# Turning q and k of four head pairs with 32x32 VectorE transposes instead of TensorE, in a retimed order of steps

## The chip, the cores and the metric

The kernel runs on one core of one Trainium2 chip. The metric is the device time of one execution in microseconds (us); lower is better. The inputs lie in device memory when the clock starts, and the output is written back there.

## What is computed

Attention with a sliding window and a few sink keys, followed by a two-layer MLP. Shapes: q, k and v are 4 batches x 8 heads x 768 positions x 64 in 32-bit floats; the weights are 512 x 2048 and 2048 x 512 in 64-bit floats; the output is 3072 x 512.

```python
scores = scale * np.matmul(q, k.transpose(0, 1, 3, 2))      # scale = 1/8
keep = is_sink | in_window                                  # 4 sinks, window of 128
scores = np.where(keep, scores, -1000000000.0)
a = np.exp(scores - max); a = a / (sum + 1e-09)
x = np.matmul(a, v)                                         # heads side by side: 3072 x 512
h = x @ w_in
out = (h * sigmoid(h)) @ w_out
```

## The kernel before, in words

**Chunks and pairs.** The 3072 rows are cut into 8 chunks of 384 rows (half a batch, three blocks of 128). Attention for a chunk runs in four *pairs* of heads; pair `p` belongs to chunk `p // 4`, so pairs 0 to 3 make chunk 0's input to the MLP and pairs 4 to 7 make chunk 1's. The first two chunks are both first halves of a batch, and they (`FP=8`, so pairs 0 to 7) go through a path of its own in 32-bit floats; the functions of that path begin with `f_`. All later pairs use hi/lo splits in the fp32r type, in `q_prep`, `k_prep`, `scores` and so on; those functions are not touched.

**The float32 path of a pair**, with head `j` = 0 or 1:

- `f_load` (line 629): four DMAs on SyncE's queue bring q and k in as 128 positions by 64 columns, in runs of 256 bytes.
- `f_prep` (line 667): TensorE turns q and k with 128x128 transposes into the PSUM tiles `qt` and `kt` (L673, six per pair). ScalarE copies them into SBUF: `kT` (L684) and two halves of `qT` (L687). `qT` is one of two long-lived tiles, `qlf` for even pairs and `qdf` for odd ones, in which head j's 64 partitions hold q and the others zeros. VectorE copies eight sink columns into `kT` (L688). For pairs 4 to 7 `qt` and `kt` take two of the three PSUM banks with the tag `at`.
- `f_scores(p, j)`: three matmuls per head (L720, "s" below), each followed by a masked maximum on VectorE (L727) that writes the tile `pm`.
- `f_softmax(p, j)`: three exponentials on ScalarE (L742), a sum's reciprocal on VectorE (L746, L747), three scalings (L753, on ScalarE for all but the first pair).
- `f_ptrans(p, j)`: six TensorE transposes of the probabilities (L765 to L770, tiles `pa` and `pb`), copied out into `pTz` by ScalarE (L771, L776) and VectorE (L772, L774).
- `f_av(p, j)`: three matmuls with v (L788, tile `o`); behind the second head ScalarE and VectorE split the result into `xh` and `xl` (L795, L796), which is what the MLP reads.

**The MLP of a chunk** goes over 16 slices of 128 hidden columns. Slice `fc` has twelve matmuls (L852, tile `h`, two PSUM buffers), then `act` (ScalarE makes `gh` at L863 and `sg` at L864, VectorE `gl` at L866), then nine matmuls into three output banks (L878 to L880, tiles `out`). L863 needs another ScalarE table than L742, so going from the one to the other costs an ACT_TABLE_LOAD.

**Weights.** They come in as 64-bit words, in 32 tiles of 512 KB: four groups of eight (four of w_in, four of w_out), group g serving the hidden slices 4g to 4g+3 of every chunk. Each tile is turned into a 32-bit float by three VectorE passes (L41, L42, L43, tile `wcv`), rounded into the hi part by ScalarE (L826) and the lo part taken by VectorE (L828; the first few on GpSimd). The raw tiles share two buffers, and `wcv` shares its buffers with `gh` and `gl`. All of this lies in the first 140 us, over the attention of pairs 0 to 7 and chunk 0's MLP.

**What sets the order.** Each step is put into a list with a time from the table `OPT`, and the steps are recorded in the order of these times. One unit is one hidden slice of the MLP. `S` is the start of the MLP, `F1` the delay of pairs 4 to 7 behind it, `s1` their spacing, `f_p` the lead of `f_prep`, `f_pt` that of `f_ptrans`, `w[g]` the start of weight group g, `m0` chunk 0's offset of `act`, and `a` the offsets of the later pairs. A list scheduler then fixes each engine's queue; every engine works its own queue strictly in order, as does SyncE with its DMAs, which wait there for their buffers.

Of the kernel before, what the change touches and what calls it, by code (L numbers as in the profile page):

```python
# [8 lines left out]
F32 = mybir.dt.float32  # L9
# [11 lines left out]
NS = 8  # L21
SEG = 128 + NS
# [2 lines left out]


OPT = dict(
    S=7.901, s0=0.903, f_l=2.468, f_p=-1.643, f_v=3.079, f_sm=0.693, f_pt=0.795, f_av=0.251,
    tk=15.973, s1=1.65, F1=1.024, D0=2.076, w=[0.458, 8.623, 11.237, 18.573], wd=[0.85, 0.58,
    1.293, 0.67], wc=19.252, wcd=2.681, warm=7, wg=4, ord=1, edge=8, dua=15, adp=0, glp=0,  # L30
    ptv=7, fill=[0, 4, 0, 0, 1, 0, 0, 2], na=[2, 16], lod=[6, 32], nv=[0, 0], hid=[0, 0],
    ktd=[0, 0], a=dict(load=-3.44, q=0.257, k=-0.012, v=1.813, s=1.461, sd=0.613, sm=1.795,
    smd=0.605, pt0=2.725, st=3.866, pt1=3.355, av0=4.289, av1=4.669), m0=dict(act=0.108,
    m2=1.206), m=dict(act=1.068, m2=1.546), fin=0.927, FP=8,
)


# [132 lines left out]
def attn_moe_kernel(  # L170
# [11 lines left out]
    nc = tc.nc  # L182
    B, H, S, D = q.shape
# [5 lines left out]
    P = 128  # L189
    HP = H // 2  # L190
    CT = 384
    NTB = CT // P
# [37 lines left out]
    with ExitStack() as fast:  # L230
# [59 lines left out]
        zero = {}  # L290
# [341 lines left out]
        def f_load(p):  # L632
            c, b, half, hp = geo(p)
            s = st[p]
            for x in ("qn", "kn"):
                if p < HP and p % 2:
                    s[x] = p2.tile([P, NTB, 2, D], F32, tag="sg", name=f"{x}{p}")
                else:
                    s[x] = p1.tile([P, NTB + (x == "kn"), 2, D], F32, tag=x, name=f"{x}{p}")
            for x, src in (("qn", q), ("kn", k)):  # L640
                for j in range(2):
                    nc.sync.dma_start(
                        s[x][:, :NTB, j, :],
                        src[b, 2 * hp + j, 0:CT].rearrange("(t p) d -> p t d", p=P),
                    )

        def f_load_v(p):
            c, b, half, hp = geo(p)
# [10 lines left out]
        def bank(p, early, name):  # L659

            if p < HP:
                pool, tag = (ps_h, "h") if early == "h" else (ps_o, early)
            else:
                pool, tag = ps_a, "at"
            return pool.tile([P, 512], F32, tag=tag, name=f"{name}{p}")

        def f_prep(p):
            s = st[p]
            qt = bank(p, "o0", "qt")
            kt = bank(p, "o1", "kt")  # L670
            for src, dst in ((s["qn"], qt), (s["kn"], kt)):
# [311 lines left out]
        D0 = O["D0"]  # L983
# [51 lines left out]
```

## Time and profile before

| | |
|---|---|
| median of 2 runs | 723.79 us (722.8 to 724.79) |
| the profiled execution | 723.66 us, of which the span from first to last instruction is 721.8 us |
| TensorE (PE) busy | 705.0 us of the span, 98% |
| ScalarE (ACT) busy | 489.4 us, 68% |
| VectorE (DVE) busy | 481.3 us, 67% |
| GpSimd (POOL) busy | 281.5 us, 39% |
| granted TensorE clock | 0.998 of full speed |

A busy share is a mean over stages with different limits. For this change the stage from 40 to 150 us counts, in which pairs 4 to 7, chunk 0's MLP and the weight conversion run side by side. A matmul's shown duration holds its pipeline's depth too; what it costs TensorE in a row of others is the step from one start to the next.

### The profile page before, as it was taken

To read this page: it belongs to the slowest core of one execution; us is meant where nothing else is said; L and a number is where in the kernel's file an instruction comes from. 1 tells how busy PE (TensorE), PEld (TensorE's weight loads), DVE (VectorE), ACT (ScalarE), POOL (GpSimd) and SP (SyncE) were. 2 spreads that over 40 slices of the span, in tenths; PEclk is the share of its full clock that TensorE was granted. 3 is DMA by queue.
4 is the path that set the end of the run, shared out by engine and by line. 5 is a ranking of instruction groups with operands and counts; after the bars stand their busy time and mean duration, and the time that the engine had idled before them with its cause. 6 is when DMAs were issued, how large, how long until landed. Compare 5 with 4: busy or idle time off the path is not lost.

```text
span 721.8 us, 12275 instructions
## 1 busy us (share of the span) xinstructions
PE 705.0 (98%) x3842; PEld 624.1 (86%) x3842; DVE 481.3 (67%) x1323; ACT 489.4 (68%) x1165; POOL 281.5 (39%) x667
## 2 busy tenths in 40 slices
PE   6998999999999999999999999999999999999997
PEld 4676778798999999999999999999999999998986
DVE  5899767976776687667866777767866776731111
ACT  4889788786776777777666777777667876732112
POOL 3310000055655666444555455544554554430000
PEclk9999999999999999999999999999999999999999
DMA  7556546434522262114521353114412321001001
GB/s 180 176 154 186 148 112 173 151 84 107 147 43 40 70 187 63 22 39 138 138 41 27 84 166 66 35 34 120 136 27 41 106 58 35 1 1 45 0 1 46
DMA packets 141334, 61.86 MB, mean 86 GB/s; under 512 B 130001, under 2 KB 130001, under 8 KB 141265
## 3 DMA queue, kind: packets, MB, share of 16 engines
q1 hardware_dynamic: 140976, 61.04, 32.9%
q8 instruction: 31, 0.51, 0.3%
q14 instruction: 39, 0.31, 0.1%
q10 hardware_dynamic: 288, 0.00, 0.0%
HBM read 54.72 MB, written 6.29 MB: 85 GB/s over the span
## 4 chain that ended last, share of the span: by engine, by line
PE 81%; DMA 5%; DVE 5%; ACT 3%; POOL 2%; issue 2%; SPq 1%; DVEq 0%; POOLq 0%; ACTq 0%
PE h L852 32%; PE out L880 11%; PE out L879 11%; PE out L878 11%; PE o L575 4%; DMA wraw<-in_moe_w_in_dram 3%; PE o L788 2%; PE s L468 2%; PE s L464 2%; PE pt L520 2%; DMA wraw<-in_moe_w_out_dram 2%; PE o L591 1%; DVE wcv L43 1%; DVE wcv L42 1%; PE o L584 1%
## 5 line engine op out<-in xcount | busy, mean ns | idle before, releaser
L852 PE MATMUL h<-xh,winh 128*128 128x384 f32 x512 | 177.2, 346 | 0.0
L852 PE MATMUL h<-xh,winl 128*128 128x384 f32 x512 | 173.9, 340 | 0.0
L852 PE MATMUL h<-xl,winh 128*128 128x384 f32 x512 | 172.7, 337 | 0.0
L878 PE MATMUL out<-wouth,gh 128*128 128x512 f32 x384 | 153.2, 401 | 1.7 <-ACT gh L863 1.6
L879 PE MATMUL out<-woutl,gh 128*128 128x512 f32 x384 | 151.8, 396 | 0.5 <-DVE woutl L828 0.3
L880 PE MATMUL out<-wouth,gl 128*128 128x512 f32 x384 | 150.2, 396 | 0.0
L863 ACT ACTIVATE gh<-h 128x384 fp32r<-128x384 f32 x128 | 62.9, 492 | 104.4 <-PE h L852 100.7
L866 DVE TENSOR_TENSOR gl<-sg,gh 128x384 fp32r<-128x384 f32 x128 | 75.4, 589 | 87.2 <-ACT sg L864 84.9
L852 PEld LDWEIGHTS h<-xh,winh 128*128 128x128 f32 x512 | 96.3, 188 | 3.0 <-issue 0.9
L852 PEld LDWEIGHTS h<-xl,winh 128*128 128x128 f32 x512 | 96.5, 189 | 2.1
L852 PEld LDWEIGHTS h<-xh,winl 128*128 128x128 f32 x512 | 96.2, 188 | 0.5 <-issue 0.3
L880 PEld LDWEIGHTS out<-wouth,gl 128*128 128x128 f32 x384 | 71.8, 188 | 17.2 <-DVE gl L866 0.6
L878 PEld LDWEIGHTS out<-wouth,gh 128*128 128x128 f32 x384 | 72.2, 188 | 14.4 <-ACT gh L863 2.4
L879 PEld LDWEIGHTS out<-woutl,gh 128*128 128x128 f32 x384 | 72.1, 188 | 13.2 <-DVE woutl L828 1.3
L505 POOL TENSOR_SCALAR pm<-pm,r 128x128 f32<-128x128 f32 x144 | 61.5, 442 | 42.5 <-DVE r L490 39.2
L485 ACT ACTIVATE pm<-pm,mx 128x264 f32<-128x264 f32 (+1 forms) x144 | 70.6, 492 | 1.3 <-DVE mx L472 0.3
L440 POOL TENSOR_TENSOR vs<-vn,vs 128x256 fp32r<-128x256 f32 (+1 forms) x48 | 33.3, 695 | 91.4 <-ACT vs L438 78.2
L864 ACT ACTIVATE sg<-h 128x384 f32<-128x384 f32 x128 | 62.5, 488 | 0.5
L472 DVE CUSTOM_DVE_ANT_0 pm<-s,m 128x264 f32<-128x264 f32 (+1 forms) x144 | 52.9, 411 | 11.9 <-PE s L468 11.6
L600 DVE TENSOR_TENSOR x<-o,x 64x512 f32<-64x512 f32 x48 | 32.8, 683 | 35.5 <-ACT x L599 34.4
L419 POOL CAST ks<-ksA 128x24 fp32r<-128x24 f32 (+1 forms) x24 | 4.8, 201 | 131.7 <-PE s L468 73.0
L438 ACT CAST vs<-vn 128x256 fp32r<-128x256 f32 (+1 forms) x48 | 18.6, 388 | 50.1 <-PE o L584 49.6
(162 smaller groups left out, 1337.7 us busy)
## 6 DMA issues: line engine op xcount, KB each, us to landing
wraw<-in_moe_w_in_dram SPq DMA_DIRECT2D x16, 512.0 KB
wraw<-in_moe_w_out_dram SPq DMA_DIRECT2D x16, 512.0 KB
wchk<-in_moe_w_in_dram SPq DMA_DIRECT2D x16, 512.0 KB
wchk<-in_moe_w_out_dram SPq DMA_DIRECT2D x16, 512.0 KB
qn<-in_q_dram SPq DMA_DIRECT2D x96, 48.0 KB
kn<-in_k_dram SPq DMA_DIRECT2D x64, 64.0 KB
vn<-in_v_dram SPq DMA_DIRECT2D x32, 128.0 KB
out_dram<-ost SPq DMA_DIRECT2D x7, 512.0 KB
```

The source lines that it names most:

```text
L440: nc.gpsimd.tensor_tensor(vs[:, j0:, j, 1, :], vn[:, j0:, j, :], vs[:, j0:, j, 0, :], ALU.subtract)
L472: nc.vector.tensor_tensor_reduce(out=pm[:, t, off:], in0=sp[:, :w], in1=(m0, m1, m2)[min(blk, 2)], scale=-0.125, scalar=3.0e38, op0=ALU.ad ...
L485: nc.scalar.activation(x, x, AF.Exp, bias=mx[:, p, j * NTB + t : j * NTB + t + 1], scale=-1.0, accum_out=r[:, t : t + 1],)
L505: nc.gpsimd.tensor_scalar(x, x, r[:, t : t + 1], 1.0, ALU.mult, ALU.mult)
L600: nc.vector.tensor_tensor(x32[:, :n], o[0:64, :n], x32[:, :n], ALU.add)
L852: nc.tensor.matmul(hps[:, :CT], w[g][:, cc, fs], s[x], start=n == 0, stop=n == 3 * NCC - 1)
L863: nc.scalar.activation(gh, hps[:, :CT], AF.Silu)
L864: nc.scalar.activation(sg, hps[:, :CT], AF.Silu)
L866: eng.tensor_tensor(gl, sg, gh, ALU.subtract)
L878: nc.tensor.matmul(o, gh[:, ts_], wout_h[g][:, f], start=fc == 0, stop=False)
L879: nc.tensor.matmul(o, gh[:, ts_], wout_l[g][:, f], start=False, stop=False)
L880: nc.tensor.matmul(o, gl[:, ts_], wout_h[g][:, f], start=False, stop=fc == NFC - 1)
```

## The change

Pairs 4 to 7 (`ft=[4, 8]`) load q and k with eight DMAs instead of four, each of 32 partitions, so that a 32x32 block of q lies on 32 partitions; the runs are 128 bytes instead of 256. VectorE's transpose, which turns each 32x32 block by itself, then writes `kT` and the two halves of `qT` directly. The TensorE transposes, the PSUM tiles `qt` and `kt` and the three ScalarE copies of these pairs are gone, and the copy of the eight sink columns goes from VectorE to GpSimd. Pairs 0 to 3 keep the old preparation. The table of times has new numbers: among others `S` 7.901 to 8.269, `F1` 1.024 to 2.394, `f_p` -1.643 to -1.822, `f_pt` 0.795 to 0.73, `w[1]` 8.623 to 9.414, `m0`'s `act` 0.108 to 0.421.

```diff
 OPT = dict(
-    S=7.901, s0=0.903, f_l=2.468, f_p=-1.643, f_v=3.079, f_sm=0.693, f_pt=0.795, f_av=0.251,
-    tk=15.973, s1=1.65, F1=1.024, D0=2.076, w=[0.458, 8.623, 11.237, 18.573], wd=[0.85, 0.58,
+    S=8.269, s0=0.903, f_l=2.468, f_p=-1.822, f_v=3.079, f_sm=0.693, f_pt=0.73, f_av=0.251,
+    tk=15.766, s1=1.65, F1=2.394, D0=2.076, w=[0.458, 9.414, 11.237, 18.573], wd=[0.85, 0.58,
...
             for x, src in (("qn", q), ("kn", k)):
                 for j in range(2):
-                    nc.sync.dma_start(
-                        s[x][:, :NTB, j, :],
-                        src[b, 2 * hp + j, 0:CT].rearrange("(t p) d -> p t d", p=P),
-                    )
+                    if not OPT["ft"][0] <= p < OPT["ft"][1]:
+                        nc.sync.dma_start(
+                            s[x][:, :NTB, j, :],
+                            src[b, 2 * hp + j, 0:CT].rearrange("(t p) d -> p t d", p=P),
+                        )
+                        continue
+
+                    s[x, "b"] = s[x].rearrange("p t h d -> p (t h d)")[:, :CT]
+                    for e in range(2):
+                        to = slice(64 * j + 32 * e, 64 * j + 32 * e + 32)
+                        nc.sync.dma_start(
+                            s[x, "b"][to].rearrange("p (i d) -> p i d", d=32),
+                            src[b, 2 * hp + j, 0:CT, 32 * e : 32 * e + 32].rearrange(
+                                "(i t) d -> t i d", t=32
+                            ),
+                        )
...
         def f_prep(p):
             s = st[p]
+            if OPT["ft"][0] <= p < OPT["ft"][1]:
+                qT = zero["qd" if p % 2 else "ql"]
+                kT = p1.tile([P, NTB, SEG], F32, tag="x32" if p % 2 else "ks", name=f"kT{p}")
+                s["qT"], s["kT"] = qT, kT
+                nc.vector.transpose(
+                    kT[:, :, :P], s["kn", "b"].rearrange("p (t c) -> p t c", c=P)
+                )
+                for j in range(2):
+                    rows = slice(64 * j, 64 * j + 64)
+                    nc.vector.transpose(qT[rows, j], s["qn", "b"][rows])
+                nc.gpsimd.tensor_copy(kT[:, 1, P:], kT[:, 0, :NS])
+                return
```

The table changes each engine's queue at many places in the first 150 us. Three of them follow, as the built programs have them; the number behind a tile's name tells buffers apart, and in `s_1_0` or `pa_4` the digits are pair or head and part.

TensorE, around the first output slice of chunk 0, before (the row with `out_0` is the first matmul that waits for `gh` of slice 0):

```order
L720 MATMUL s_1_2_716<-kT_600,qlf 128x264
L765 MATMUL pa_4_793<-ident,pm_0_637 128x128
L766 MATMUL pa_4_793<-ident,pm_0_637 128x128
L768 MATMUL pb_0_794<-ident,pm_0_637 128x128
L767 MATMUL pa_4_793<-ident,pm_0_637 8x128
L769 MATMUL pb_0_794<-ident,pm_0_637 128x128
L770 MATMUL pb_0_794<-ident,pm_0_637 128x128
L720 MATMUL s_0_0_841<-kT_662,qdf 128x128
L720 MATMUL s_0_0_841<-kT_662,qdf 128x256
L878 MATMUL out_0_750<-wouth_133,gh_0_698 128x512
```

The same place after the change, where `o_915` is pair 4's first product with v and `pa_4_951`, `pb_1_952` are the probabilities of its second head:

```order
L744 MATMUL s_0_2_890<-kT_681,qdf 128x264
L812 MATMUL o_915<-pTz_151,vn_616 64x384
L812 MATMUL o_915<-pTz_151,vn_616 64x256
L812 MATMUL o_915<-pTz_151,vn_616 64x128
L789 MATMUL pa_4_951<-ident,pm_1_753 128x128
L790 MATMUL pa_4_951<-ident,pm_1_753 128x128
L791 MATMUL pa_4_951<-ident,pm_1_753 8x128
L792 MATMUL pb_1_952<-ident,pm_1_753 128x128
L793 MATMUL pb_1_952<-ident,pm_1_753 128x128
L794 MATMUL pb_1_952<-ident,pm_1_753 128x128
L902 MATMUL out_0_715<-wouth_133,gh_0_676 128x512
```

More of pair 4's attention now stands ahead of the first output slice.

VectorE, around pair 4's first maxima, before (`wcv` is a weight tile, `s_0_0_638` pair 4's first scores):

```order
L688 COPY kT_600<-kt_593 128x8
L43 SCALAR_TENSOR_TENSOR wcv_0_631<-wraw_0_629,wcv_0_631 128x512
L828 TENSOR_TENSOR woutl_134<-wcv_7_607,wouth_133 128x512
L796 TENSOR_TENSOR xl_617<-o_577,xh_616 128x384
L828 TENSOR_TENSOR winl_136<-wcv_0_631,winh_135 128x512
L727 ISA pm_0_637,mx<-s_0_0_638,m_94 128x128
```

After the change, where the transposes of pair 5 (`qdf`) already stand between pair 4's steps:

```order
L852 TENSOR_TENSOR woutl_134<-wcv_7_588,wouth_133 128x512
L690 STREAM_TRANSPOSE qdf<-qn_627 64x384
L820 TENSOR_TENSOR xl_598<-o_571,xh_597 128x384
L751 ISA pm_0_666,mx<-s_0_0_667,m_94 128x128
L751 ISA mx 128x1
L41 TENSOR_SCALAR wcv_0_621<-wraw_0_619 128x512
L751 ISA pm_0_666,mx<-s_0_0_667,mf 128x256
```

The first tile of weight group 1 (`wcv_0`) went from ahead of pair 4's maxima to between them.

SyncE's queue, from the load of pair 4's v on, before:

```order
L654 DMA vn_620<-in_v_dram 128x3x64 x2
L802 DMA wraw_0_629<-in_moe_w_in_dram 128x1024
L802 DMA wraw_1_646<-in_moe_w_in_dram 128x1024
L642 DMA qn_623<-in_q_dram 128x3x64 x2
L642 DMA kn_624<-in_k_dram 128x3x64 x2
L802 DMA wraw_2_667<-in_moe_w_in_dram 128x1024
```

And after:

```order
L666 DMA vn_616<-in_v_dram 128x3x64 x2
L652 DMA qn_627<-in_q_dram 32x12x32 x2
L826 DMA wraw_0_619<-in_moe_w_in_dram 128x1024
L652 DMA qn_627<-in_q_dram 32x12x32
L652 DMA kn_628<-in_k_dram 32x12x32 x4
L826 DMA wraw_1_637<-in_moe_w_in_dram 128x1024
L826 DMA wraw_2_658<-in_moe_w_in_dram 128x1024
```

Pair 5's loads are twice as many, in smaller blocks, and stand partly ahead of the weight tiles that they followed.

More of the change, by code (lines that the diff above doesn't have):

```diff
@@ L27 @@
 OPT = dict(
-    S=7.901, s0=0.903, f_l=2.468, f_p=-1.643, f_v=3.079, f_sm=0.693, f_pt=0.795, f_av=0.251,
-    tk=15.973, s1=1.65, F1=1.024, D0=2.076, w=[0.458, 8.623, 11.237, 18.573], wd=[0.85, 0.58,
+    S=8.269, s0=0.903, f_l=2.468, f_p=-1.822, f_v=3.079, f_sm=0.693, f_pt=0.73, f_av=0.251,
+    tk=15.766, s1=1.65, F1=2.394, D0=2.076, w=[0.458, 9.414, 11.237, 18.573], wd=[0.85, 0.58,
     1.293, 0.67], wc=19.252, wcd=2.681, warm=7, wg=4, ord=1, edge=8, dua=15, adp=0, glp=0,
     ptv=7, fill=[0, 4, 0, 0, 1, 0, 0, 2], na=[2, 16], lod=[6, 32], nv=[0, 0], hid=[0, 0],
-    ktd=[0, 0], a=dict(load=-3.44, q=0.257, k=-0.012, v=1.813, s=1.461, sd=0.613, sm=1.795,
-    smd=0.605, pt0=2.725, st=3.866, pt1=3.355, av0=4.289, av1=4.669), m0=dict(act=0.108,
-    m2=1.206), m=dict(act=1.068, m2=1.546), fin=0.927, FP=8,
+    ktd=[0, 0], a=dict(load=-3.44, q=0.257, k=-0.36, v=1.782, s=1.198, sd=0.6, sm=1.795,
+    smd=0.605, pt0=2.69, st=3.866, pt1=3.355, av0=4.346, av1=5.057), m0=dict(act=0.421,
+    m2=1.206), m=dict(act=1.068, m2=1.546), fin=0.93, FP=8, ft=[4, 8],
 )
```

## The prediction

> **What bounds the kernel now.** I read the page first, then the span cut into stages, then who waits for whom where TensorE has gaps, and last the order in time there.
>
> ```profile
> PE   6998999999999999999999999999999999999997
> DVE  5899767976776687667866777767866776731111
> ACT  4889788786776777777666777777667876732112
> ```
>
> TensorE is busy nearly throughout, so the end moves by TensorE's work and by its gaps, and the gaps lie in the first fifth. There VectorE and ScalarE come nearest to full. The windows (busy us of each engine, count in brackets, granted clock, DMA share, GB/s) show it by stage:
>
> ```profile
> core 0: us, PE busy (x) PEld busy (x) DVE busy (x) ACT busy (x) POOL busy (x), PEclk, DMA share, GB/s
> 0.00:42.30 42.30, 34.75 (x172) 24.45 (x172) 32.00 (x123) 28.87 (x86) 15.69 (x27) 0.96 0.61 165
> 42.30:64.40 22.10, 19.80 (x108) 15.09 (x106) 19.84 (x57) 19.37 (x46) 0.00 (x0) 1.00 0.71 192
> 64.40:152.30 87.90, 86.73 (x443) 70.04 (x444) 69.11 (x173) 73.15 (x165) 4.78 (x11) 1.00 0.51 142
> 152.30:650.00 497.70, 497.03 (x2794) 455.19 (x2793) 349.86 (x954) 352.57 (x836) 261.07 (x629) 1.00 0.30 73
> ```
>
> Stage A is 42.3 to 64.4 us, from the first MLP matmul to the output matmuls of hidden slice 1. Stage B goes on to those of slice 15, at 152.3. In A three engines are each busy for 19.4 to 19.8 of 22.1 us: a chain through all three, with ScalarE what TensorE waits for:
>
> ```profile
> PE out L878 <- ACT gh L863: 1.6, 2, 1.1
> PE pa L765 <- ACT pm L753: 0.6, 1, 0.6
> ```
>
> From 152.3 on TensorE is busy for 497.03 of 497.70 us. The order of its rows there is the same in both programs but for one exchanged pair, so I add nothing behind B. Ahead of A TensorE's order differs only in pairs 2 and 3, whose transposes stand three matmuls earlier.
>
> **The change part by part.** First the prices on TensorE, from starts in the timeline:
>
> ```profile
> 31.31 1.27 PE L720 MATMUL s<-kT,qlf 128*128 128x128 f32 x6
> 32.64 1.51 PE L788 MATMUL o<-pTz,vn 128*64 128x384 f32 x6
> 34.08 0.33 PE L765 MATMUL pa<-ident,pm 128*128 128x128 f32 x1
> 52.91 0.49 PE L673 MATMUL qt<-ident,qn 128*128 128x128 f32 x3
> 53.24 0.49 PE L673 MATMUL kt<-ident,kn 128*128 128x128 f32 x3
> 53.57 0.60 PE L720 MATMUL s<-kT,qlf 128*128 128x128 f32 x3
> 60.58 0.34 PE L852 MATMUL h<-xh,winh 128*128 128x384 f32 x1
> 60.76 0.34 PE L852 MATMUL h<-xl,winh 128*128 128x384 f32 x1
> 70.94 0.40 PE L878 MATMUL out<-wouth,gh 128*128 128x512 f32 x1
> 71.18 0.39 PE L879 MATMUL out<-woutl,gh 128*128 128x512 f32 x1
> ```
>
> Three transposes step by 0.33, so 0.11 each; a hidden matmul 0.175, an output one 0.235, the scores of a head 1.2 (1.33 shown to the next start, of which I give some 0.1 to the change to another kind of matmul), a product with v 1.44, a group of six probability transposes 0.65.
>
> *Removed from TensorE:* 24 transposes x 0.11 = 2.6 us, half of them in A and half in B, where TensorE itself sets the pace.
>
> *Removed from ScalarE, added to VectorE:*
>
> ```profile
> L684 ACT COPY kT<-kt 128x384 f32<-128x384 f32 x4 | 1.9, 476 | 0.0
> L687 ACT COPY qdf<-qt 64x384 f32<-64x384 f32 x4 | 1.9, 474 | 0.0
> L687 ACT COPY qlf<-qt 64x384 f32<-64x384 f32 x4 | 1.9, 473 | 0.0
> L688 DVE COPY kT<-kt 128x8 f32<-128x8 f32 x4 | 0.6, 162 | 0.5 <-ACT kT L684 0.4
> L390 DVE STREAM_TRANSPOSE qt<-qn x24: 539/551/594, 142.7 to 613.5; 128x384 f32<-128x384 f32 x24
> ```
>
> ScalarE loses 5.7 us over four pairs. VectorE gains three transposes per pair. The nearest row is the same transpose of 384 columns into PSUM, 551 ns. SBUF to SBUF, and on 64 partitions, is not in this trace. Below, an exchange at the pace of L41 (421 ns for 512 columns, quoted further down) would be 0.32; above, the slowest L390 is 0.59. I take 0.55, of which 0.07 overlaps the next instruction: 0.48 x 12 = 5.8 us, less 0.4 for L688. The copy of eight columns goes to GpSimd, idle in A; the scores' third matmul waits for it, a cost between 0 and some 0.2 (L688's 162 ns), beside the two matmuls ahead.
>
> [...]
>
> *Moved:* in A the new order does more. Ahead of slice 1's output it adds the scores of pair 5's second head (1.2), two products with v (2.88) and one group of probability transposes (0.65), and loses 12 transposes (1.3). TensorE's own work (36 hidden matmuls 6.3, nine output ones 2.1, and the attention) rises from 18.2 to 21.6 us, still under 22.1. VectorE decides. Its prices are these, less the 0.07 between a duration and the next start:
>
> ```profile
> L43 DVE SCALAR_TENSOR_TENSOR wcv<-wraw,wcv 128x512 int32<-128x512 int32 x26 | 17.9, 687 | 0.4
> L42 DVE SCALAR_TENSOR_TENSOR wcv<-wraw,wcv 128x512 int32<-128x512 int32 x25 | 17.1, 684 | 0.4
> L41 DVE TENSOR_SCALAR wcv<-wraw 128x512 int32<-128x512 int32 x25 | 10.5, 421 | 6.2 <-DMA wraw<-in_moe_w_in_dram 3.6 <-PE out L879 1.6 <-DMA wraw<-in_moe_w_out_dram 0.8
> 41.27 0.93 DVE L42 SCALAR_TENSOR_TENSOR wcv<-wraw,wcv 128x512 int32<-128x512 int32 x1
> 50.61 0.55 DVE L796 TENSOR_TENSOR xl<-o,xh 128x384 fp32r<-128x384 f32 x1
> 51.08 0.68 DVE L828 TENSOR_TENSOR winl<-wcv,winh 128x512 fp32r<-128x512 f32 x1
> 51.68 0.28 DVE L727 CUSTOM_DVE_ANT_0 pm<-s,m 128x128 f32<-128x128 f32 x1
> 64.84 0.55 DVE L866 TENSOR_TENSOR gl<-sg,gh 128x384 fp32r<-128x384 f32 x1
> ```
>
> From 41.3 to the end of slice 1's `gl`, before: 20 passes over weight tiles 11.6, six lo parts 3.7, three sets of maxima (0.9 each) 2.7, `xl` and `gl` four times 0.48, small ones 1.6; together 21.6, and the rows end at 65.4, so 2.5 us were idle. After: 24 passes 13.8, seven lo parts 4.3, four sets 3.6, five `xl` and `gl` 2.4, six transposes 2.9, small ones 2.1; together 29.1. Ahead of 41.3 two transposes (0.96) come in and one L41 (0.4) moves behind: +0.6. With no idle VectorE ends `gl` of slice 1 at 41.3 + 0.6 + 29.1 = 71.0. It waits less than before, since more stands in its queue, but it still waits once per head for ScalarE's exponentials; I take 1.9 of the 2.5: 72.9. Slice 1's output starts two matmuls ahead of that: A ends at 72.4 in place of 64.4. ScalarE, relieved of half its 5.7 us of copies there, stands behind VectorE's maxima.
>
> B then lasts 87.9, less the 4.7 that moved into A, less 12 transposes (1.3): 81.9. It also gets calmer: slices 3 to 7 run with almost no attention between them, and TensorE changes between 32-bit and fp32r matmuls 48 times instead of 57 in A and B, at the 0.1 a change from above. Of that and of B's waits for ScalarE
>
> ```profile
> PE out L878 <- ACT gh L863: 1.1, 1, 1.1
> PE s L720 <- ACT pTz L776: 0.5, 1, 0.5
> ```
>
> I count 1.3 as gone: 80.6. If the moved attention has not left ScalarE's way by slice 8, where pairs 6 and 7 now crowd with their table loads, that 1.3 is not won.
>
> *DMA:* the loads go from 16 to 32 issues, about 0.45 each on SyncE's queue (the middle row of the next fence is one), 7 us in all in a queue that mostly waits for buffers. The small runs cost transfer time; ahead of 8 us the queue moved 256-byte runs, around 164 us 128-byte ones:
>
> ```profile
> 4.00:8.00 4.00, 2.07 (x11) 1.36 (x10) 2.70 (x14) 1.79 (x3) 0.97 (x4) 1.00 1.05 226
> 161.33 0.42 SPq L362 DMA_DIRECT2D kn<-in_k_dram  x1
> 160.00:168.00 8.00, 7.45 (x44) 6.84 (x43) 5.88 (x11) 4.49 (x11) 4.54 (x12) 1.00 0.36 61
> ```
>
> 226 / 1.05 is 215 GB/s at full share, 61 / 0.36 is 169. A pair's 393 KB take 1.8 or 2.3 us: 0.5 more, 2 us over four pairs, at most all on the path, at least none. I take none: the DMA share is 0.71 in A and 0.51 in B, and weight tiles wait for their buffers.
>
> *Sum:* A ends at 72.4, B at 72.4 + 80.6 = 153.0, against 152.3. The profiled execution took 723.66 (721.8 of span and 1.9 around it), 0.13 under the median of the runs, so 723.66 + 0.7 = **724.4 us**: TensorE's 2.6 us are won and given back at VectorE.
>
> **The rivals.**
>
> 1. *The attention out of the way: faster.* If VectorE hardly waits (A ends at 70.5) and B loses another 2 us of its waits, the end is 70.5 + 78.6 = 149.1, 3.2 earlier: 720.5. For it: ScalarE, which TensorE waited for, has 5.7 us less; `qt` and `kt` no longer take two of three PSUM banks. Against it: VectorE is the busier of the two in A already, 19.84 against 19.37.
> 2. *VectorE becomes the bound: slower.* The maxima stand behind weight passes and transposes in one queue, ScalarE's exponentials behind the maxima, `gh` behind the exponentials. It decides once VectorE's idle in A passes 4 us or the transposes cost more than 0.55: then A ends at 74.8, and if B keeps its old waits, 74.8 + 81.9 = 156.7, 4.4 later: 728.1. For it: 29 us of work in a row. Against it: before, the same chain left only 2.5 us idle. [...]
> 3. *Small runs starve the weights.* All 2 us of the DMA term on the path: 726.4. Before, L41 waited 3.6 + 0.8 us for weight tiles, but little of that in A.
>
> **How the numbers follow.** My forecast, no change that could be measured (722 to 726), gets 0.42; the first rival 0.27, the second 0.24, the third 0.05, something larger 0.02. The low bound takes the first rival with transposes at 0.32 (six in A x 0.2 = 1.2 less): 719. The high bound takes the second with the 2 us of DMA: 730. A measurement of this kernel tells about 2% from no change, 14.5 us. A gain of that size would need all 2.6 us and nearly every gap of A and B, 1%; a loss that size needs a stall no row shows, 3%; so 0.01, 0.96, 0.03.
>
> **What would show it.** Right, if slice 1's output starts near 72 and slice 15's near 153, VectorE's idle in A is 1 to 3 us, a transpose takes 0.5 to 0.6 us, and the span behind slice 15 stays within 1 us. Wrong, if slice 15's output comes before 150 or after 156, if the waits of TensorE in slices 8 to 15 grow past 3 us, or if L41 or the transposes wait for DMA by more than 2 us in A.

## The result, and the profile after

| | before | after | after, timed a second time |
|---|---|---|---|
| median of the runs, us | 723.79 | 734.09 (733.15 and 735.03) | 733.03 (732.23 to 733.52, four runs) |
| ratio to before, 95% interval | | 1.0142 (1.0119 to 1.0165) | 1.0123 (1.0106 to 1.0140) |
| profiled execution, us | 723.66 | 735.03 | 733.52 |
| its span, us; mean granted clock | 721.8; 0.998 | 733.2; 0.989 | 731.8; 0.990 |
| TensorE busy, us | 705.0 | 709.7 | 708.2 |

The change costs about 1.3%, 9 to 10 us. It is inside the 2% that a measurement tells from no change, but above the range given, which ended at 730. The page after, in 40 slices of 18.3 us:

```profile
PE   7997899999999999999999999999999999999997
DVE  5898877867776668766876778766876776731111
ACT  4868559877677767667777867667777867642112
PEclk9999899999999999999999999999999999999999
```

The fourth and fifth slices of PE read 7 and 8 where 8 and 9 stood before, and the clock has an 8 in the fifth. ScalarE reads 5 and 5 in the fifth and sixth (7 and 8 before), then 9 and 8 (8 and 7): some of its work has moved back. The windows of after, cut at the same events as the prediction's stages (A ends at 76.4, B at 165) and with B in parts; columns as there:

```profile
core 0: us, PE busy (x) PEld busy (x) DVE busy (x) ACT busy (x) POOL busy (x), PEclk, DMA share, GB/s
42.30:76.40 34.10, 26.03 (x123) 17.55 (x121) 29.43 (x83) 26.42 (x70) 1.95 (x3) 0.94 0.62 156
76.40:88.00 11.60, 11.55 (x43) 9.99 (x44) 9.10 (x18) 5.44 (x13) 0.50 (x1) 0.73 0.70 184
88.00:100.00 12.00, 12.00 (x62) 10.72 (x61) 9.32 (x17) 3.40 (x7) 0.00 (x0) 1.00 0.42 108
100.00:120.00 20.00, 19.45 (x103) 15.39 (x102) 15.63 (x41) 16.88 (x34) 1.25 (x4) 1.00 0.59 156
120.00:130.00 10.00, 9.20 (x47) 7.50 (x46) 7.13 (x20) 9.34 (x18) 0.00 (x0) 1.00 0.60 134
130.00:143.00 13.00, 11.61 (x48) 8.78 (x47) 9.86 (x26) 11.61 (x25) 0.31 (x1) 0.87 0.44 146
143.00:165.00 22.00, 21.59 (x113) 17.33 (x112) 15.75 (x40) 16.15 (x41) 2.87 (x7) 1.00 0.32 82
165.00:650.00 485.00, 485.00 (x2731) 444.47 (x2730) 347.00 (x946) 348.71 (x828) 261.68 (x630) 1.00 0.31 76
```

From 165 on TensorE is full, as it was from 152.3 before. All of the loss lies ahead. In A TensorE is idle for 8.1 of 34.1 us, and the granted clock falls under 1 in three windows. TensorE's rows at the ends of the stages, with the idle time ahead and what ended it in brackets:

```profile
57.35 0.33 PE L789 MATMUL pa<-ident,pm 128*128 128x128 f32 x1 [2.34 <-ACT pm L777]
76.45 0.80 PE L902 MATMUL out<-wouth,gh 128*128 128x512 f32 x1 [5.14 <-ACT gh L887]
...
164.87 0.39 PE L902 MATMUL out<-wouth,gh 128*128 128x512 f32 x1
```

A ends at 76.45 (64.4 before) and B at 164.87 (152.3 before). Behind the second gap an output matmul takes 0.80 us, at 164.87 it takes 0.39. Windows cut behind the two gaps, and around a third place, show why:

```profile
57.20:61.00 3.80, 3.38 (x12) 1.65 (x12) 2.55 (x12) 3.69 (x13) 0.19 (x1) 0.71 0.64 168
...
76.40:80.50 4.10, 4.05 (x9) 2.98 (x10) 3.19 (x8) 3.43 (x9) 0.00 (x0) 0.50 0.51 140
80.50:83.00 2.50, 2.50 (x10) 2.42 (x9) 2.50 (x6) 0.00 (x0) 0.00 (x0) 0.56 0.93 259
...
133.90:136.80 2.90, 1.51 (x6) 0.62 (x5) 2.61 (x7) 2.58 (x4) 0.00 (x0) 1.00 0.53 175
136.80:141.00 4.20, 4.20 (x14) 3.59 (x15) 2.65 (x6) 4.14 (x10) 0.00 (x0) 0.59 0.37 129
```

The windows' clocks are means. Cut into windows of 0.4 us, the clock of after reads 0.50 from 59.2 to 62.0, from 76.0 to 82.4 and from 137.6 to 140.4 us, 0.51 to 0.84 in the windows at the edges of these stretches, and 1.00 otherwise from 56 to 64, 74 to 86 and 134 to 144 us. Read as a clock that is either whole or half, twice the missing share is the time at half clock: 0.06 of the 34.1 us of A, 0.27 of 11.6 and 0.13 of 13.0 behind it. That is some 13.7 us: 3.4 us behind the first gap, 6.8 behind the long one and 3.4 at 137 us.

A short gap does not always bring it. The run `early_gh` (below) has the first gap too, 2.4 us long, and the clock stays whole. The rows for 54 to 64 us, of after and then of early_gh with its wait:

```profile
54.00:64.00 10.00, 7.30 (x29) 3.74 (x27) 8.69 (x32) 8.86 (x27) 0.19 (x1) 0.83 0.44 98
```

```profile
54.00:64.00 10.00, 5.57 (x28) 3.06 (x26) 8.41 (x31) 8.91 (x26) 0.19 (x1) 1.00 0.44 103
PE pa L833 <- ACT pm L821: 2.4, 1, 2.4
```

In five profiles with after's order the rows show a gap of 2.0 to 2.4 us at this place and the clock behind it: in one of them no half clock follows (early_gh), in three some 3.4 us of it (after, after_lo, after_both), in one (after_mul) some 6.8. So a short gap's length alone does not tell what it costs; what else decides was not shown. Behind a gap of 4.3 to 6.0 us half clock followed in all eight profiles whose rows show one.

Over the whole span TensorE's idle time went from 16.8 to 23.5 us (+6.7) and its busy time from 705.0 to 709.7 (+4.7). The 2.6 us of transposes did leave, so 7.3 us of busy time came in. The half clock is some 5.1 of them: fill2 (below), in which the clock is whole through A and B, is busy for 711.7 us, of which its dummy matmuls are 7.1, so for 704.6 without them.

### The profile page after: what moved, and what is told of

It reads as the page before. It is cut to its first block, busy times and chain, and to the rows that moved or that the text cites. A ratio compares the mean times of both kernels' runs of the same rounds, so it can differ in the third digit from the quotient of the medians.

```text
span 733.2 us, 12244 instructions
## 1 busy us (share of the span) xinstructions
PE 709.7 (97%) x3818; PEld 626.9 (85%) x3818; DVE 488.5 (67%) x1331; ACT 484.8 (66%) x1153; POOL 283.1 (39%) x671
## 4 chain that ended last, share of the span: by engine, by line
PE 86%; DVE 5%; DMA 3%; ACT 2%; SPq 1%; issue 1%; POOL 0%; ACTq 0%; DVEq 0%
PE h L876 35%; PE out L902 12%; PE out L903 12%; PE out L904 12%; PE o L575 4%; PE s L464 2%; PE s L468 2%; PE pt L520 2%; DMA wraw<-in_moe_w_in_dram 2%; PE o L812 1%; DVE wcv L43 1%; PE o L591 1%; PE o L584 1%; DMA wraw<-in_moe_w_out_dram 1%; ACT pm L766 1%
## 5 line engine op out<-in xcount | busy, mean ns | idle before, releaser
L902 PE MATMUL out<-wouth,gh 128*128 128x512 f32 x384 | 155.5, 405 | 5.9 <-ACT gh L887 5.9
L902 PEld LDWEIGHTS out<-wouth,gh 128*128 128x128 f32 x384 | 72.7, 189 | 18.3 <-ACT gh L887 6.6
L904 PEld LDWEIGHTS out<-wouth,gl 128*128 128x128 f32 x384 | 72.2, 189 | 18.3 <-DVE gl L890 1.4
L903 PEld LDWEIGHTS out<-woutl,gh 128*128 128x128 f32 x384 | 72.9, 190 | 12.3
L505 POOL TENSOR_SCALAR pm<-pm,r 128x128 f32<-128x128 f32 x144 | 63.2, 455 | 37.4 <-DVE r L490 37.4
L540 POOL TENSOR_SCALAR_AFFINE_SELECT pq<-pq 128x384 fp32r<-128x384 f32 (+1 forms) x96 | 49.8, 518 | 6.3
L536 POOL TENSOR_SCALAR_AFFINE_SELECT pq<-pq 128x384 fp32r<-128x384 f32 (+1 forms) x96 | 49.4, 514 | 6.2 <-ACT pq L529 4.4
```

Of the source, the lines that this page charges most:

```text
L505: nc.gpsimd.tensor_scalar(x, x, r[:, t : t + 1], 1.0, ALU.mult, ALU.mult)
L536: nc.gpsimd.affine_select(out=before, in_=own, pattern=[[0, n], [-1, P]], compare_op=ALU.is_gt, fill=0.0, base=0, channel_multiplier=1,)
L540: nc.gpsimd.affine_select(out=own, in_=own, pattern=[[0, n], [1, P]], compare_op=ALU.is_ge, fill=0.0, base=0, channel_multiplier=-1,)
L902: nc.tensor.matmul(o, gh[:, ts_], wout_h[g][:, f], start=fc == 0, stop=False)
L903: nc.tensor.matmul(o, gh[:, ts_], wout_l[g][:, f], start=False, stop=False)
L904: nc.tensor.matmul(o, gl[:, ts_], wout_h[g][:, f], start=False, stop=fc == NFC - 1)
```

## The experiments

Six theories were tried; the letters are those of the expectations. *VectorE* (V, V'): its longer queue ahead of slice 1's output sets the end of A. *Place* (1, P): it is the place of `gh` in ScalarE's queue. *Clock* (2): a gap of TensorE costs its own length and then half clock behind it. *Crowd* (S): pairs 6 and 7, pushed back, meet ScalarE at its limit between 100 and 152 us. *Loads* (L; the prediction's third rival): the 128-byte runs and their doubled issues. *Order* (3, O): the new numbers of the table, and not the new path for q and k. "Order held" means that each engine's instructions keep the order of the kernel named, with only the edit put in its place; without that, an edit moves the scheduler's order at many other places.

### Which half of the change costs

`path_only`: the new path with the old numbers. `order_only`: the new numbers with the old path.

```diff
 path_only (to before)              order_only (to after)
+ ft=[4, 8]                         - ft=[4, 8]
+ the branch in f_load and f_prep   + ft=[0, 0]
```

> The new path for q and k with the old order numbers (the scheduler still moves attention forward by itself, since the transposes leave TensorE). Theory 1, the loss is made in stage A by what stands ahead of a slice's gh in ScalarE's queue, not by the price of the transposes: gh of slice 0 here stands behind two more sets of exponentials than in the changed kernel, gh of slice 1 close behind it; a stall of 4 to 8 us ahead of slice 0's output in place of slice 1's, and some 728 to 736 us. Rival, the new numbers alone are at fault: the old ones give 720 to 724 us.

> The new order numbers with the old path (transposes on TensorE, copies on ScalarE, 256-byte loads). Theory 1: gh of slice 1 again stands behind four weight casts and a set of exponentials, so a stall of 2 to 5 us ahead of slice 1's output, and 725 to 731 us. Rival, the transposes on VectorE and their small loads cost the 10 us: 722 to 725 us and no wait of TensorE for gh over 1.5 us.

Measured: path_only 734.68 us, 1.0150 (1.0125 to 1.0174); order_only 735.83, 1.0160 (1.0133 to 1.0187), more than either theory expected of it. Each half alone costs as much as both. The costs don't add, so "path or order" was the wrong question. Why order_only loses was not traced. VectorE's sum of work is not the reason there: no transpose of pairs 4 to 7 stands on it, and from 42.3 us to slice 1's output, at 74.03, VectorE is busy for 24.18 of 31.73 us and ScalarE for 24.67. In path_only the scheduler also ordered the rest anew, so three runs held the order of before. `path_pinned` exchanges the path alone; `runs_pinned` is before with the second chunk's q and k loads cut in two (128-byte runs, 32 issues); `path_big` is path_pinned with 16 loads of 256-byte runs, which leaves the second chunk's q and k mixed up.

```diff
 runs_pinned, for pairs 4 to 7
-nc.sync.dma_start(s[x][:, :NTB, j, :], src[b, 2 * hp + j, 0:CT]...)
+for e in range(2):
+    ds_ = slice(32 * e, 32 * e + 32)
+    nc.sync.dma_start(s[x][:, :NTB, j, ds_], src[b, 2 * hp + j, 0:CT, ds_]...)
```

> The kernel before with its order held on every engine, and only the path of q and k exchanged: 24 transposes leave TensorE, 12 copies ScalarE, 4 small copies VectorE; three transposes per pair stand on VectorE 4 to 8 places ahead of where the small copy stood; the copies of eight columns go to GpSimd; 32 loads of 128-byte runs stand where the 16 were. Theory 3, the order that the scheduler makes of the kernel costs the 10 us and the path itself nothing: 720 to 725 us, slice 1's output at 63 to 66 us and no gap of TensorE over 2 us behind 54 us. Rival, the path (VectorE's 5.4 us more in its fullest stage, or the small loads) costs it: 727 to 734 us.

> The kernel before with its order held and the loads of q and k of the second chunk alone changed: each is cut into two of half the columns, 128-byte runs, 32 issues instead of 16; the tiles and all that reads them stay. Every theory but the third rival of the prediction expects 723 to 725 us; that one (2 us of transfer on the path) 725 to 727.

> The run with the path in the old order, order held, but with the loads of before: 16 issues of 256-byte rows into the same tiles. VectorE turns them all the same, so q and k of the second chunk are mixed up and only the times count. In that run VectorE waited 3.2 us for kn of pair 5 and 1.8 us for a weight tile behind pair 7's loads. Theory L, the loads of 128-byte runs make those waits and the half clock after them: both go and the time is 721 to 727 us. Theory V, VectorE's 12 transposes in a full queue are what costs: 729 to 734 us.

Measured: runs_pinned 726.5, 1.0036 (1.0018 to 1.0054); path_pinned 733.47, 1.0133 (1.0114 to 1.0153); path_big 729.2, 1.0091 (1.0073 to 1.0109). The path costs 9.5 us with the order held, so the *order* theory is not the whole account. In the old order the small loads cost 0.0036 x 724 = 2.6 us by themselves, and 9.5 − 5.8 = 3.7 of the path's 9.5 us. The other 5.8 is the exchange itself, with the transposes at these places of VectorE's queue (4 to 8 ahead of the old small copy); other places were not tried. The split is rough, since in path_big a transpose reads columns of both heads and so waits for both heads' loads. Where the exchange sits, in SyncE's queue and on VectorE; first before, then path_pinned, then path_big:

```profile
43.45 3.84 SPq L802 DMA_DIRECT2D wraw<-in_moe_w_in_dram  x2
...
49.61 0.96 SPq L642 DMA_DIRECT2D kn<-in_k_dram  x2
```

```profile
43.63 5.37 SPq L891 DMA_DIRECT2D wraw<-in_moe_w_in_dram  x2
...
51.05 2.79 SPq L708 DMA_DIRECT2D kn<-in_k_dram  x4
...
55.42 0.58 DVE L743 STREAM_TRANSPOSE kT<-kn 128x384 f32<-128x384 f32 x1 [3.15 <-DMA kn<-in_k_dram]
```

```profile
51.13 1.02 SPq L706 DMA_DIRECT2D kn<-in_k_dram  x2
...
55.44 0.58 DVE L741 STREAM_TRANSPOSE kT<-kn 128x384 f32<-128x384 f32 x1 [2.08 <-DMA kn<-in_k_dram]
```

With the transposes on VectorE, the two weight tiles ahead of q and k spend 5.37 us in SyncE's queue in place of 3.84 (5.37 in path_big too), so k is issued 1.4 to 1.5 us later. Then VectorE itself waits for k, with the maxima queued behind: TensorE waits 3.4 us for `pm`, and the first output slice comes at 63.4 in path_pinned and in path_big alike, 58.4 before. The two stay alike up to 81.4 us; their difference arises behind that, where path_pinned has a wait of 2.54 us and half clock after it (three output matmuls take 1.65 us at 88.21), path_big one of 1.66 and the whole clock (0.91 us for three at 86.68). On TensorE the transposes had no maxima behind them. That the weight issues wait longer because VectorE frees `wraw` later is argued from the rows, not tried.

### What sets stage A

Four runs with after's order held. `after_tr2` does each transpose twice. `after_notr` puts plain copies on GpSimd in their place, so q and k of the second chunk are not turned. `after_big` has 16 whole loads, which mixes q and k up. `after_lo` moves the eight lo parts of weight group 1 from VectorE to GpSimd, and `before_lo` does so in before.

```diff
 after_tr2                              after_lo, before_lo
 nc.vector.transpose(to, x)            -nc.vector.tensor_tensor(lo, cf, hi, ALU.subtract)
+nc.vector.transpose(to, x)            +nc.gpsimd.tensor_tensor(lo, cf, hi, ALU.subtract)
 after_notr: nc.vector.transpose -> nc.gpsimd.tensor_copy
```

> The changed kernel, order held, with each of the 12 transposes issued twice in a row (the second writes the same again): 12 x 0.49 = 5.9 us more on VectorE, six of them, 2.9 us, before slice 1's output. Theory V: slice 1's output 2 to 4 us later and the end 2 to 6 us later, 736 to 740 us. Theory L or O, VectorE has room there: 734 to 735.5 us.

> The changed kernel, order held, without VectorE's 12 transposes: plain copies on GpSimd, which stands idle there, take their place (so q and k of the second chunk are not turned, and the scores are of other numbers). Theory V: 3 us of VectorE's work go out of the stage before 76 us, gh of slice 1 starts 2 to 4 us earlier, and the end comes 3 to 6 us earlier, 728 to 731 us. Theory L or O: 732 to 735 us.

> The changed kernel, every engine's order held, with 16 loads of 256-byte rows in place of 32 of 128-byte runs into the same tiles (q and k of the second chunk are mixed up by it, the work on every engine is the same). Theory L: the weight tiles come sooner, VectorE's wait of 1.1 us at 69 us and those of 3.5 us between 100 and 160 shrink, and the end comes 3 to 7 us earlier, 727 to 731 us. Theory V or O (VectorE's queue, or the order alone): 732 to 735 us.

> The changed kernel, order held, with the eight lo parts of weight group 1 (0.61 us each, six of them between 54 and 78 us) moved from VectorE to GpSimd, which stands idle there and takes 1.27 us for one. Theory V', VectorE is the bound ahead of slice 1's output and of slices 2 and 3: slice 1's output starts 2 to 4 us earlier, slice 3's 3 to 5 us, and the end 2 to 5 us, 729 to 732 us. Theory P, it is the place of gh and gl in the two queues and the buffers they wait for, not VectorE's sum: 733 to 736 us.

> The kernel before, order held, with the eight lo parts of weight group 1 on GpSimd instead of VectorE. Theory V' (VectorE bounds that stage in every order of this kernel): part of the 4 us that TensorE stands idle between 42 and 170 us goes, 720.5 to 723 us. Otherwise 723 to 725 us, or slower if the longer lo parts hold the two shared buffers.

Measured: after_tr2 736.37, 1.0173 (1.0153 to 1.0193); after_notr 736.41, 1.0184 (1.0167 to 1.0201); after_big 736.55, 1.0189 (1.0172 to 1.0206); after_lo 735.71, 1.0179 (1.0162 to 1.0196); before_lo 724.83, 1.0023 (1.0012 to 1.0033).

after_tr2 speaks for VectorE. Six more transposes ahead of slice 1, 6 x 0.49 = 2.9 us, move its output by 79.44 − 76.45 = 2.99 (2.6 against the second profile of after, where it comes at 76.85):

```profile
79.44 0.80 PE L948 MATMUL out<-wouth,gh 128*128 128x512 f32 x1 [6.00 <-ACT gh L933]
...
42.30:79.40 37.10, 26.05 (x123) 18.45 (x123) 33.26 (x92) 26.86 (x70) 1.96 (x3) 0.91 0.54 143
```

TensorE's and ScalarE's busy time in the stage stayed (26.05 and 26.86 us); VectorE's rose to 33.26 of 37.1. Work added to VectorE passes on nearly one to one to the end of A; of the 5.9 us added in all, some 2 to 4 reach the end of the kernel (1.0173, where after has 1.0142 and 1.0123). Holding the order is no change by itself: in after_mul, whose edit lies behind 100 us, A ends at 76.63.

Taking work away did not pay, each time for a reason of its own. In after_notr slice 1 came 3.3 us later, at 79.76, though VectorE is busy for only 26.89 us from 42.3 to there (29.43 in after up to 76.4). The buffers of q and k come free when GpSimd is done with them, SyncE waits 8.0 us for its copies of pair 4, and a weight tile behind that lands late:

```profile
50.08 0.43 DVE L81 TENSOR_SCALAR wcv<-wraw 128x512 int32<-128x512 int32 x1 [3.30 <-DMA wraw<-in_moe_w_out_dram]
```

In after_big it came at 78.37, where a transpose waits for its loads:

```profile
69.57 0.57 DVE L745 STREAM_TRANSPOSE qlf<-qn 64x384 f32<-64x384 f32 x1 [2.79 <-DMA qn<-in_q_dram]
```

Here too a transpose waits for both heads' loads, which it does not in after, so this run can't say what the 128-byte runs cost in the new order. The *loads* theory holds in the old order; in the new one it is open. after_notr and after_big both end later than any theory had it. In after_lo slice 1 came at 76.36, 0.09 earlier, though VectorE has the group's lo parts no more. Two of VectorE's passes beside GpSimd's work took longer; the rows of both engines:

```profile
64.38 2.86 POOL L907 TENSOR_TENSOR winl<-wcv,winh 128x512 fp32r<-128x512 f32 x2 [7.30 <-ACT winh L904]
66.50 1.03 DVE L81 TENSOR_SCALAR wcv<-wraw 128x512 int32<-128x512 int32 x1
69.78 1.26 POOL L907 TENSOR_TENSOR winl<-wcv,winh 128x512 fp32r<-128x512 f32 x1 [2.54 <-ACT winh L904]
69.94 1.65 DVE L82 SCALAR_TENSOR_TENSOR wcv<-wraw,wcv 128x512 int32<-128x512 int32 x1
```

The same passes take 0.42 and 0.68 us without a neighbour; why they take longer beside GpSimd was not shown. With that, VectorE's busy time from 42.3 to 76.4 fell by only 0.9 us, from 29.43 to 28.54, and that became waiting. In before_lo the same move costs 1.8 us: no relief there either. More work on VectorE delays A, then, but less of it did not bring A forward, and no way to relieve VectorE in A without a side effect was found. It is shown to be part of the chain, not to be the whole bound.

Two runs moved slice 1's activation. `early_gh` (order held, a buffer of its own for slice 1's `gh`) puts its `gh` and `sg` ahead of the fourth `winh` cast and its `gl` ahead of a weight tile's passes; slice 2's `gh` and `sg` move up to slice 1's old place. `act_back` sets m0's `act` from 0.421 back to 0.108, without the order held.

```diff
 act_back                              early_gh, order on ScalarE
-m0=dict(act=0.421, m2=1.206)           gh_1, sg_1, winh cast 4 of group 1, ...
+m0=dict(act=0.108, m2=1.206)          (was: winh cast 4, ..., gh_1, sg_1)
```

> The changed kernel with every engine's order held but for slices 1 and 2: both Silu passes of slice 1 stand ahead of the fourth winh cast on ScalarE, its gl ahead of the weight pass at 69.97 us on VectorE (both engines waited there, for 1.5 and 1.1 us), those of slice 2 take slice 1's old place; gh of slice 1 has a buffer of its own. Nothing is added or removed. Theory 1, the 5.1 us are a matter of the place in ScalarE's queue: slice 1's output starts at 71 to 72 us, no half clock follows it, and the end comes 5 to 9 us earlier, 725 to 729 us. Rival, VectorE's sum of work is the bound and the stall only moves on to slices 2 to 4: 731 to 734 us.

> The changed kernel with one number of the old table, 0.108 instead of 0.421 for the place of the Silu passes of chunk 0's slices; the scheduler makes its own order of it, in which slice 0's gh stands ahead of the first winh cast and slice 1's ahead of the first cast of the next group, but slice 0's output now ahead of pair 5. Theory 1, the place of gh in ScalarE's queue makes the loss: 724 to 730 us and no wait of TensorE for gh over 3 us. Rival, VectorE's sum of weight passes, maxima and transposes is the bound, whatever the order: 731 to 736 us, with the wait moved to another operand.

Measured: early_gh 733.75, 1.0140 (1.0115 to 1.0165); act_back 736.80, 1.0178 (1.0159 to 1.0197). In early_gh slice 1's output came at 71.00, 5.4 us earlier, and the stall stands one slice on:

```profile
81.36 0.80 PE L950 MATMUL out<-wouth,gl 128*128 128x512 f32 x1 [4.72 <-DVE gl L936]
```

Slice 3 then starts at 87.51, against 87.86. So the place of `gh` sets slice 1's time, but not the end: the wait now has another name. Slice 2's `gl` was left where it was: it shares two buffers with weight words that are handed out in the old sequence. In act_back slice 1's output came at 72.70, 3.75 us earlier, and the end was not earlier (span 734.2, after 733.2; the median, 736.80, is a little above the rival's range). The windows of act_back show where that went:

```profile
88.00:100.00 12.00, 9.97 (x47) 8.40 (x48) 9.70 (x18) 3.53 (x7) 0.00 (x0) 1.00 0.43 115
100.00:120.00 20.00, 18.43 (x95) 14.29 (x93) 13.42 (x36) 14.05 (x28) 1.22 (x4) 1.00 0.56 151
120.00:143.00 23.00, 20.51 (x96) 16.80 (x96) 18.94 (x44) 21.71 (x44) 0.00 (x0) 0.93 0.55 156
```

From 88 to 143 TensorE is idle for 6.1 us, in after for 2.7. So an earlier end of A alone is not a gain either: the same work then waits in B. What slice 1 waits for and when A ends are a place where the loss shows, not its cause.

### What the clock and the crowd are worth

`fill` and `fill2` put dummy matmuls with f32 operands into the gaps at 54 and 71 us (10 and 20, then 5 and 10; the ones into `out` add zeros). `after_mul` moves 12 multiplications of pairs 6 and 7 (units 12 to 15; a unit is one head of a pair) from ScalarE to GpSimd. `after_both` joins after_mul and after_lo, `fill_mul` joins fill2 and after_mul; `after_again` is after once more. Order held but for after_again.

```diff
 fill2 (fill: 10 and 20)
+if (p, j) == (4, 0): for _ in range(5):  matmul(pa, ident, m1, start=True, stop=True)
+if (c, fc) == (0, 1): for _ in range(10): matmul(out, nought, m1, start=False, stop=False)
 after_mul, units 12 to 15
-nc.scalar.mul(x[t], x[t], r[:, t : t + 1])
+the same on nc.gpsimd
```

> The changed kernel with every engine's order held, and TensorE kept at work in its two long gaps: 10 matmuls of 264 columns that are overwritten ahead of pair 4's first probability transposes, and 20 that add zero ahead of slice 1's output matmuls (0.23 us each, 2.3 and 4.7 us, inside gaps of 2.3 and 5.1 us). Nothing else changes; the output is the reference's. Theory 2, about half of the loss is the half granted clock that follows the gaps (3.4 and 6.8 us long, at 58.8 and 75.9): both stretches go and the end comes 3 to 5 us earlier, 729 to 731 us. Rival, the low clock costs nothing because ScalarE and VectorE are behind anyway: 733 to 735 us, slice 1's output where it was and waits for gh longer in slices 2 to 6.

> As the run before with matmuls in TensorE's two gaps, now with half as many: a 32-bit matmul of 264 columns took 0.44 us there (4.61 us for ten), so the gaps of 2.3 and 5.1 us were overfilled by 1.6 and 4.3 us. Here 5 and 10 of them, 2.2 and 4.4 us; orders held, output the reference's. Theory 2, the half clock behind the gaps costs about 1.7 + 3.1 us: slice 1's output starts where it did or up to 1.7 us earlier (75 to 76.5), slice 3's at 83.5 to 85 instead of 87.9, and the end comes 3 to 5 us earlier, 729 to 731 us. Rival, ScalarE and VectorE set the pace behind the gaps and the low clock is hidden: slice 3's output at 87 to 88, the end at 733 to 735 us.

> The changed kernel, order held, with the twelve multiplications by 1/r of pairs 6 and 7 (1.2 us a head) moved from ScalarE to GpSimd. Between 100 and 152 us ScalarE holds all of pairs 6 and 7 with 12 table loads (8 in the kernel before, where three more stand between 76 and 100). Theory S, ScalarE is the bound there and makes the second loss (waits at 134 us and a half clock behind them): 4.8 us go from it and the end comes 2 to 4 us earlier, 730 to 732.5 us, with no wait over 0.3 us and no half clock between 130 and 142. Otherwise 733.5 to 736 us.

> The two moves together. Theories V' and S: the gains add, 726 to 730 us. If only one of them holds: 729 to 732 us. If neither: 733 to 736 us.

> The changed kernel, order held, with both repairs that helped: 5 and 10 matmuls that keep TensorE at work in its two long gaps, and the multiplications of pairs 6 and 7 on GpSimd. If the half clock behind the gaps and ScalarE's crowd between 100 and 152 us are two losses of their own, the gains add: 2 to 2.5 us and 2 to 3 us, 729 to 731 us, and no half clock is left. If the later loss only takes back what the first repair gains: 732 to 733 us.

> The changed kernel once more, timed in the same rounds as the next run, so that the two can be set against each other: 733 to 736 us by every theory.

| kernel | median, us | ratio (95%) | span | clock |
|---|---|---|---|---|
| fill | 735.63 | 1.0162 (1.0139 to 1.0186) | 733.0 | 0.994 |
| fill2 | 732.36 | 1.0119 (1.0094 to 1.0144) | 730.7 | 0.998 |
| after_mul | 732.37 | 1.0134 (1.0117 to 1.0151) | 730.3 | 0.989 |
| after_both | 733.80 | 1.0154 (1.0137 to 1.0171) | 732.2 | 0.989 |
| fill_mul | 730.71 | 1.0096 (1.0079 to 1.0113) | 728.0 | 0.996 |
| after_again | 733.03 | 1.0123 (1.0106 to 1.0140) | 731.8 | 0.990 |

In fill the dummies were too long, and held the real work up:

```profile
71.91 9.17 PE L771 MATMUL out<-m,nought 128*128 128x264 f32 x40
```

Half as many fit, and the clock stayed whole. The row of fill2 for the stretch behind the long gap:

```profile
76.40:80.50 4.10, 3.86 (x20) 3.38 (x20) 3.28 (x6) 2.82 (x7) 0.00 (x0) 1.00 0.66 161
```

Twenty matmuls in place of 9 at 0.50. The gap is still there (the dummies do nothing), yet slice 3 starts at 85.40 and not 87.86. Not all of these 2.5 us are kept. B, from slice 1's output at 75.84 to slice 15's at 162.37, takes 86.5 us for 88.4, at a clock of 1.00 throughout, and TensorE's idle time in it rises from 3.1 to 4.4 us. So of the time at half clock most was hidden: with the clock whole, TensorE waits for ScalarE and VectorE instead. The time, 732.36, lies between the ranges of the two theories.

after_mul has the crowd's stretch at full clock:

```profile
130.00:143.00 13.00, 12.02 (x60) 9.23 (x60) 10.26 (x27) 10.66 (x23) 2.81 (x5) 1.00 0.42 133
```

Sixty matmuls in 13 us where after has 48, and 0.98 us idle in place of 1.39. The clock there is no proof for the move, since fill2 keeps 1.00 from 120 to 143 us without it, with 2.62 us idle. And behind the first gap after_mul has twice after's time at half clock, so that its mean clock is no better.

By the times neither alone is told from after: fill2's 1.0119 and after_mul's 1.0134 lie in the intervals of after's two measurements. Both together are: fill_mul's runs (729.72 to 730.95) lie wholly under after_again's (732.23 to 733.52), on one chip, 2.3 us by the medians. The profiled spans differ by 3.8 (728.0 and 731.8), but they are of the fastest run of the one and the slowest of the other. The 2.3 us are the part of the loss that was shown by taking its causes away. The other 6.7 us, 730.71 against 724.03 on that chip, stay. after_both is 1.4 us slower than after_mul, on the same chip, so the lo parts on GpSimd cost there too. No version beat before.

## Why the prediction was wrong

**The work left TensorE: right.** 24 transposes are gone. With the clock whole, fill2's TensorE is busy for 704.6 us without its dummies, where 705.0 − 2.6 would be 702.4; the 2.2 us between were not traced. The stage behind slice 15 took 568.3 us, before 569.5: no loss there. Most of that 1.2 is not the change's, since before_lo, with the old path and numbers, took 568.7.

**The transpose's price: right.** 0.55 was taken; the rows of after show 0.56 to 0.58, on 64 partitions too.

**The end of A: a term too small.** Slice 1's `gl` was to end at 72.9 and ends at 77.4; the stage ends at 76.45 in place of 72.4, 4.1 late. That VectorE's queue decides, as the second rival had it, is borne out by after_tr2 and not by the runs that took work away. The failed step is "I take 1.9 of the 2.5" for VectorE's idle time. It is 4.6 up to the end of `gl`, 2.7 more. Its work behind 41.9 us is 1.8 more than the list: one more set of maxima (0.9) stands there, and the L41 at 42.88 takes 1.20 in place of 0.42 us beside a GpSimd subtraction at 42.53. VectorE's waits there, largest first:

```profile
DVE r L770 <- ACT pm L766: 1.2, 1, 1.2
DVE wcv L41 <- DMA wraw<-in_moe_w_in_dram: 1.1, 1, 1.1
DVE xl L820 <- ACT xh L819: 0.8, 1, 0.8
DVE winl L852 <- ACT winh L850: 0.7, 1, 0.7
DVE woutl L852 <- ACT wouth L850: 0.6, 1, 0.6
```

No one wait is the cause; they are handings-over, four with ScalarE and one with SyncE's loads. "It waits less than before, since more stands in its queue" was the reason given, and it is wrong here: VectorE's rows keep the order of its queue (in path_pinned nothing of it ran in the 3.15 us for which it waited for k), so what stands behind a waiting instruction is no cover. The second rival's 74.8 for the end of A was an estimate that no run shows: VectorE's idle time did pass the rival's 4 us, no transpose of after took over 0.58, and A ended at 76.45. The end of the chain, on ScalarE and on VectorE:

```profile
68.88 0.62 ACT L850 CAST winh<-wcv 128x512 fp32r<-128x512 f32 x1 [1.50 <-DVE wcv L43]
69.51 1.28 ACT L766 ACT_TABLE_LOAD   x1
...
72.44 0.62 ACT L850 CAST winh<-wcv 128x512 fp32r<-128x512 f32 x1 [0.62 <-DVE wcv L43]
73.50 0.51 ACT L766 ACTIVATE pm<-pm,mx 128x256 f32<-128x256 f32 x1 [0.44 <-DVE mx L751]
74.62 1.28 ACT L887 ACT_TABLE_LOAD   x1
75.91 0.49 ACT L887 ACTIVATE gh<-h 128x384 fp32r<-128x384 f32 x1
```

```profile
69.97 0.43 DVE L41 TENSOR_SCALAR wcv<-wraw 128x512 int32<-128x512 int32 x1 [1.12 <-DMA wraw<-in_moe_w_in_dram]
...
72.44 0.57 DVE L690 STREAM_TRANSPOSE qlf<-qn 64x384 f32<-64x384 f32 x1
73.03 0.42 DVE L751 CUSTOM_DVE_ANT_0 pm<-s,mf 128x256 f32<-128x256 f32 x1
```

A weight tile lands 1.12 us late; VectorE's passes over it, then a transpose, then the maximum; ScalarE's exponential 0.44 behind that, a table load of 1.28, and only then `gh`, for which TensorE has stood 5.14 us. Both engines take turns at being late. That the gap is all VectorE's is not shown.

**B: waits at nothing, and no term for the clock.** It was to last 80.6 us and lasted 88.4, 7.8 more; slice 15's output at 164.87 is the prediction's own sign of being wrong (after 156). TensorE is idle for 3.1 us of B, which leaves 4.7 for the half clock; the windows at 76.40, 80.50 and 136.80 give 4.1 x 0.50 + 2.5 x 0.44 + 4.2 x 0.41 = 4.9. The sum had no term for the granted clock at all: page and windows of before showed 1.00 throughout B, where no gap is over 1.1 us. But the prediction's first window, 0 to 42.3 us, had 0.96: in before TensorE is busy for only 0.63 us from 6 to 8 us, and from 8 to 12 the clock is 0.64 and then 0.51. So the price stood in the trace. fill2 shows what the missing term is worth: with the clock whole B still lasts 86.5 us, so the clock is 1.9 of the 7.8. The larger step that failed is "I count 1.3 as gone: 80.6", which leaves B almost no waits; in fill2 they are 4.4 us. The last 1.5 us are more work of TensorE than the list had, and were not traced.

**The calm: not won.** The prediction's own condition, that pairs 6 and 7 crowd around slice 8 with their table loads, came true. ScalarE is busy for 3.40 of 12 us at 88 to 100 (10.92 before), and for 9.34 + 11.61 = 20.95 of 23 at 120 to 143 (17.13 before); of its table loads from 42 to 152 us, 12 of 15 stand behind 100 us, 8 of 16 before. TensorE's waits in B were to go, 1.2 us in before, and grew to 3.1.

**The loads at nothing: not settled.** In the order of before they cost 2.6 us alone. In the new order no run tells their cost. The third rival, at 0.05, had 2 us for them; a chance for it should have hung on where the loads stand, not on the DMA share.

**The range and the chances.** 719 to 730 left out a case in which stage A is late and something comes on top. The rival had the first of these at 728.1. With 4.1 for A, 7.8 for B and 1.2 less behind it, the sum is 724.4 + 10.7 = 735.1, for 735.03 of the profiled execution; it closes because each term is a measured difference, and does not show that the causes are separate. What stays open: which of the new numbers costs what, why the new numbers lose without the new path, and whether the same path with more room on VectorE in A would gain TensorE's 2.6 us.

## What to carry to other kernels

Where three engines are each busy for nine tenths of a stage, work taken from one and put on another is not priced by its duration: follow the receiving queue in order, with each handing-over, and ask which loads its later releases push back. Half clock followed TensorE's gap in all eight profiles here with one of 4.3 to 6.0 us, and in four of five with one of 2.0 to 2.4 us at the same place: price such a gap with what may follow it. And the end gains only what ScalarE and VectorE don't hold back: with the clock whole, B was 1.9 us shorter in fill2, and TensorE's idle time in it 1.3 us longer. And a stall that is moved is not removed: look one slice on, as early_gh shows.

## What the runs showed of the hardware

- The granted clock went to half for 3.4 us after a gap of only 2.34 us in after, for 6.8 after the same gap in after_mul, and not at all after 2.4 us in early_gh. After 5.14 us in after it was 6.8 us. With five and ten dummy matmuls in the gaps (fill2) it was 1.00 from 57.2 to 61.0 and from 76.4 to 80.5 us.
- A matmul with f32 operands and 264 columns took 0.46 us in fill (9.17 for 20 of them, two records each), so few of them fill a gap.
- Beside a GpSimd subtraction of 128x512, one of VectorE's integer passes took 1.03 us in place of 0.42 and another 1.65 in place of 0.68 (after_lo); moving eight such subtractions freed only 0.9 us of VectorE's time in A.
- Loads cut in two took more time in the queue: in path_pinned the four issues of q took 1.96 us in SyncE's queue and those of k 2.79, in path_big two whole ones 0.96 and 1.02.
